# Gated linear attention with a small MLP on one core: centring the tokens before their transposes, a first pair in chunk halves, five phase products, another order table

## The chip, the cores and the metric

The kernel runs on one core of a Trainium2 chip. The time is the device time of one execution in microseconds, the median of several runs, lower is better. The core has a matrix engine (PE), a vector engine (DVE), a scalar engine for functions (ACT), a general engine (POOL), a queue engine that issues transfers (SP), and 16 DMA engines. Each engine has its own list of instructions, in the order in which the program gives them; what another engine has to finish first is waited for with semaphores.

## The reference

```python
# q, k, v, a_re, a_im: (4, 8, 768, 48) float32;  g_ln (384), w_ch1 (384, 1536), w_ch2 (1536, 384)
mag = sqrt(a_re**2 + a_im**2);  scale = minimum(mag, 0.999) / (mag + 1e-6)
a = (a_re + 1j * a_im) * scale
for t in range(768):                       # per batch and head, S is 48 x 48 complex
    S = a[t][:, None] * S + outer(k[t], v[t])
    y[t] = q[t] @ S.real
x = y with the heads side by side          # (4, 768, 384)
mu, var = mean(x), mean((x - mu)**2)       # per token, over 384
xn = (x - mu) / sqrt(var + 1e-6) * g_ln
out = x + maximum(xn @ w_ch1, 0) @ w_ch2
```

## The kernel before, in words

The time loop is gone: the product of gates between two steps is the exponential of a difference of running sums, of log magnitudes and of phases. The work is tiled in **chunks** of 128 tokens, six to a batch, 24 in all (`n`), and in **pairs** of two chunks, 12 in all (`P`, three to a batch). One pair goes through these steps; the names are those of the order table, `P` or `n` behind the dot:

- `are`, `aim`, `k`, `q`, `vf`: loads by SP. `wl.0` to `wl.5`: the two weight matrices, in thirds, by POOL's queue.
- `ln`, `iv`, `r`, `r2`, `u`, `l`, `lc`, `th`: log magnitude and phase of each gate, on ACT, DVE and POOL. `ln`, `iv`, `u`, `e`, `en` need ACT's table of logarithm and exponential, `th`, `sin`, `cos` the one of the trigonometric functions; `tab.log` and `tab.trig` load one or the other.
- `dec`: running sums of the log magnitudes, by products with a triangle of ones (`u_e`) on PE; `e` and `en` their exponentials with either sign. `ph`: the same for the phases (`u_th`), with the phase carried over from the pair before (`car`, picked out by `pick`); `sin`, `cos` (with `abs` or, in the first three pairs, `qt` ahead of it).
- `ke`, `qe`: k and q times the exponentials, `ks`, `qs`: those times cosine (`.0`) and sine (`.1`), on DVE or POOL.
- per chunk: `kT`, `qT` (transposes on PE) with the copies `ksT`, `qsT`, or one DMA transpose by SP in place of both; `am` the attention scores, `atm` the mask on DVE; `gm`, `G` the state; `y` the output, `x` its copy; `bn` mean and variance on DVE (two instructions); `xtr`, `xT` the transpose of the tokens and its copy.
- per pair: `mm1` (first MLP layer, 36 products of 256 columns in six steps), `relu`, `rstd`; per chunk `mm2` (second layer, 12 products of 384 columns in three steps), `oa`/`ot` (scaling and residual), `st` (store).

The mean of a token is not subtracted before: it is folded into the first weight matrix. `wgc` makes a 128 x 128 tile of g/384 (`gc`), `wp` multiplies the weights by it on PE, and `wc` writes g times weight minus that product back over the weights on DVE (L392), nine pieces, before the first `mm1`.

**The order is written out by hand:** `PLAN` is a table of some 1,000 tokens `step:engine+bank`, and each engine's instructions stand in the order of that table. The rings (`RINGS`) say how many buffers each tile has. `:G@step` puts a POOL step behind a step of DVE. `warm` steps are products without a use, which keep PE busy while nothing else is ready. Helpers hide the line of many operations: L293 is any elementwise product (`tt`), L288 and L290 a copy on ACT and DVE (`put`).

Lines of the profile: L449 loads of a_re, a_im; L452 `ln`; L454 `iv`; L466 `u`; L470, L473 `l`, `lc`; L481 `dec`; L485 `e`, `en`; L489 `th`; L507 `ph`; L533 `sin`; L544, L556 `cos`; L613 `kT`, `qT`; L618 their DMA form; L636 `am`; L664 `gm`; L686, L689 `y`; L699, L700 `bn`; L707 `xtr`; L741 `mm1`; L758, L760 `relu` on ACT and DVE; L773 `mm2`; L779, L789 the scaling; L806 `warm`; L811 `tab`.

## Time and profile before

| | us |
|---|---|
| median of 3 runs | 189.33 (188.43 to 190.59) |
| the profiled execution, whole | 189.38 |
| its span | 187.7 |
| busy PE / DVE / ACT / POOL | 175.9 / 159.0 / 156.0 / 95.7 |

The profiled execution took 1.7 us more than its span, which runs from the first to the last instruction. PE's busy time counts the latency of its pipelined products, so a full PE is not one at its peak: 36 products of the first layer are 269 to 283 ns each and follow each other in 109 ns. Of the 119 `warm` products in the trace all lie in its first 33 us.

### The profile page before, as it was taken

How to read it: one execution, taken by the hardware profiler on the slowest of the kernel's cores; microseconds unless marked ns; L12 is line 12 of the kernel's file. 1: busy time of each engine (PE TensorE's matmuls, PEld its weight loads, DVE VectorE, ACT ScalarE, POOL GpSimd, SP SyncE). 2: the span in 40 equal slices, each digit the busy share in tenths (PEclk: the TensorE clock that was granted, in tenths of full speed). 3: DMA queues.
4: the chain of work that ended last, by engine and by line, in shares of the span. 5: the costliest groups of instructions: out<-in, count | busy, mean ns of one | idle time of the engine just before them, and what ended most of it. 6: DMA issues, size and time to landing. Idle time of an engine off the chain costs nothing.

```text
span 187.7 us, 5141 instructions
## 1 busy us (share of the span) xinstructions
PE 175.9 (94%) x2040; PEld 138.6 (74%) x2040; DVE 159.0 (85%) x292; ACT 156.0 (83%) x223; POOL 95.7 (51%) x117
## 2 busy tenths in 40 slices
PE   5699999999999999999999999999999899797992
PEld 3488677888677897777877877877768577685772
DVE  0599999999989999889999899968999878676463
ACT  5699999999999999999999999988999869143220
POOL 8137387776614990696068570740621507521650
PEclk9999999999999999999999999999999999999999
DMA  5999999999999895899999999999989899996423
GB/s 136 284 243 178 235 237 213 209 191 227 228 235 265 188 263 131 147 219 213 187 244 206 181 245 218 179 227 171 213 188 197 190 210 155 234 121 167 136 98 126
DMA packets 131799, 37.23 MB, mean 198 GB/s; under 512 B 125888, under 2 KB 131776, under 8 KB 131776
## 3 DMA queue, kind: packets, MB, share of 16 engines
q1 hardware_dynamic: 128272, 33.76, 86.5%
q0 software_dynamic: 2784, 2.36, 8.5%
q10 hardware_dynamic: 720, 0.79, 1.2%
q8 instruction: 16, 0.26, 0.5%
q14 instruction: 7, 0.06, 0.1%
HBM read 28.31 MB, written 4.72 MB: 176 GB/s over the span
## 4 chain that ended last, share of the span: by engine, by line
PE 56%; DVE 19%; DMA 13%; issue 3%; SPq 3%; ACT 3%; POOL 1%; DVEq 0%; ACTq 0%; POOLq 0%
PE banks L773 20%; PE banks L741 14%; DMA aim<-in_a_im_dram 5%; DMA qsT<-qs 5%; PE banks L613 5%; PE banks L507 4%; PE banks L636 3%; DVE w1b L392 3%; DVE atm L293 3%; DMA ksT<-ks 2%; PE banks L481 2%; DVE r L293 2%; PE banks L686 2%; PE banks L707 2%; PE banks L689 2%
## 5 line engine op out<-in xcount | busy, mean ns | idle before, releaser
L773 PE MATMUL banks<-w2b,h 128*128 128x384 bf16 (+1 forms) x300 | 54.6, 319 | 0.0
L741 PE MATMUL banks<-xT,w1b 128*128 128x256 bf16 x432 | 51.2, 272 | 0.1
L741 PEld LDWEIGHTS <-w1b 128*128 128x128 bf16 x432 | 41.2, 98 | 6.5 <-DVE xT L290 0.8
L773 PEld LDWEIGHTS <-h 128*128 128x128 bf16 x300 | 26.8, 97 | 12.5
L293 DVE TENSOR_TENSOR atm<-banks,mask 128x1024 bf16<-128x1024 f32 x24 | 28.9, 1219 | 4.8 <-PE banks L636 4.5
L758 ACT ACTIVATE h<-banks 128x1024 bf16<-128x1024 f32 (+1 forms) x25 | 24.9, 1006 | 9.4 <-PE banks L741 9.2
L293 POOL TENSOR_TENSOR ke<-k,en 128x384 bf16<-128x384 f32 x17 | 15.8, 933 | 16.5 <-ACT en L485 4.7
L811 ACT ACT_TABLE_LOAD x18 | 23.1, 1283 | 1.1 <-PEq L827 0.8
L806 PE MATMUL banks<-u_e 128*128 128x256 f16 x119 | 16.7, 289 | 2.5 <-POOL u_e L322 2.2
L636 PE MATMUL banks<-qsT,ksT 128*128 128x128 bf16 x192 | 14.6, 219 | 2.9 <-DMA qsT<-qs 1.8
L760 DVE TENSOR_SCALAR h<-banks 128x1024 bf16<-128x1024 f32 (+1 forms) x12 | 14.0, 1175 | 3.7 <-PE banks L741 3.6
L293 POOL TENSOR_TENSOR qe<-q,e 128x384 bf16<-128x384 f32 x13 | 12.0, 929 | 9.3 <-DVE ks L293 5.3
L636 PEld LDWEIGHTS <-ksT 128*128 128x128 bf16 x192 | 12.2, 98 | 5.0 <-issue 2.3
L806 PEld LDWEIGHTS <-u_e 128*128 128x128 f16 x119 | 12.1, 104 | 4.6 <-POOL u_e L322 1.9
L293 POOL TENSOR_TENSOR r<-aim,are 128x768 f16<-128x768 f32 x6 | 10.9, 1813 | 6.1 <-ACT are L454 5.9
L786 POOL TENSOR_TENSOR ot<-ot,x 128x384 f32<-128x384 f32 x11 | 10.6, 974 | 6.3 <-DVE x L290 4.4
L288 ACT CAST x<-banks 128x384 bf16<-128x384 f32 x16 | 7.7, 483 | 7.2 <-PE banks L689 6.4
L470 DVE SCALAR_TENSOR_TENSOR l<-r,w 128x768 f16<-128x768 f16 (+1 forms) x13 | 12.9, 996 | 0.7 <-ACT r L466 0.6
L699 DVE BATCH_NORM_STATS2 stats<-x 128x6 f32<-128x384 bf16 x24 | 13.2, 550 | 0.3 <-ACT x L288 0.3
L293 POOL TENSOR_TENSOR qs<-qe,trig 128x768 bf16<-128x768 bf16 x6 | 10.3, 1725 | 5.9 <-DVE qe L293 3.5
L418 POOL TENSOR_SCALAR v<-vf 128x768 bf16<-128x768 f32 x8 | 7.0, 869 | 12.0 <-DMA vf<-in_v_dram 7.0
L686 PE MATMUL banks<-v,atm 128*128 128x48 bf16 x192 | 12.1, 183 | 0.2 <-DVE atm L293 0.2
(100 smaller groups left out, 385.0 us busy)
## 6 DMA issues: line engine op xcount, KB each, us to landing
k<-in_k_dram SPq DMA_DIRECT2D x24, 192.0 KB, 4.3
q<-in_q_dram SPq DMA_DIRECT2D x24, 192.0 KB, 4.5
vf<-in_v_dram SPq DMA_DIRECT2D x24, 192.0 KB, 4.1
are<-in_a_re_dram SPq DMA_DIRECT2D x11, 384.0 KB, 4.6
aim<-in_a_im_dram SPq DMA_DIRECT2D x11, 384.0 KB, 4.6
out_dram<-ot SPq DMA_DIRECT2D x20, 192.0 KB, 3.1
w1b<-in_moe_w_ch_dram POOLq DMA_DIRECT2D x3, 384.0 KB, 6.1
w2b<-in_moe_w_ch_dram POOLq DMA_DIRECT2D x3, 384.0 KB, 7.2
```

The costliest lines, as they stand in the source:

```text
L293: {"DVE": nc.vector, "POOL": nc.gpsimd}[eng(name)].tensor_tensor(**kw)
L470: nc.vector.scalar_tensor_tensor(out=S_("l"), in0=S_("r2"), scalar=0.5, in1=S_("w"), op0=ALU.mult, op1=ALU.add)
L636: nc.tensor.matmul(ps[:, h], lhsT=T("ksT", n)[:, h], rhs=T("qsT", n)[:, h], start=True, stop=True)
L686: nc.tensor.matmul(ps[:, h], lhsT=T("atm", n)[:, h], rhs=T("v", P)[:, c, h], start=True, stop=nfirst)
L699: nc.vector.bn_stats(out=T("stats", n), in_=T("x", n))
L741: nc.tensor.matmul(ps[:, jj], lhsT=w1b[:, dc, ts(gi * JG + jj, C)], rhs=T("xT", P)[:, dc].rearrange("p c t -> p (c t)"), start=(dc == 0), ...
L758: act(out=dst, in_=src, func=AF.Relu)
L760: nc.vector.tensor_scalar(out=dst, in0=src, scalar1=0.0, scalar2=None, op0=ALU.max)
L773: nc.tensor.matmul(bank(own)[:, 0:w], lhsT=T("h", P)[:, j, ts(c, C)], rhs=w2b[:, j, es], start=(j == 0), stop=(j == NJ - 1))
L786: nc.gpsimd.tensor_tensor(out=T("ot", n)[:, es], in0=T("ot", n)[:, es], in1=T("x", n)[:, es], op=ALU.add)
L806: g.add(f"warm.{i}", lambda i=i: nc.tensor.matmul(bank(f"warm.{i}")[:, 0:256], lhsT=u_e[:, 0, 0], rhs=u_e[:, 1].rearrange("p j t -> p (j t ...
L811: g.add(f"tab.{nm}.{i}", lambda tab=tab: nc.scalar.preload_act_table_set(tab))
```

## The change

1. **Centring.** A new step `xc` subtracts the token's mean (`mv`, from `bn`) from `x`, on DVE or POOL, and `xtr`/`xT` transpose `xc` in place of `x`. So a chunk's transpose now needs its `bn`. The weights are only scaled by g (`wg`, three instructions for each third: `wg.1` on DVE, `wg.0` on ACT, `wg.2` on POOL); `cmean`, `gc`, `wgc`, `wp` and `wc` are gone.
2. **Pair 0 by chunk.** Its two parts were heads 0 to 3 and 4 to 7; now they are chunk 0 and chunk 1. Its a_re and a_im come in runs of 192 bytes (384 before); its running sums take 3 and 5 products of 384 columns (8 and 12 of 192 before); its first layer is in 6 steps of 12 products of 128 columns, each with a `relu` of its own.
3. **Five phase products.** In pairs 1 to 11 one of the six products of `ph` is saved: a new step `tc` copies 64 rows of the phases into the tile of the carried phase, and one product with a joint matrix (`u_car`) does for two.
4. **A new order table.** 65 `warm` products of 256 columns and 57 of 512 (`warmw`) in place of 119 of 256. DMA transposes 28 in place of 25. Steps move between engines: for example `ks` is on DVE 16 times and on POOL 10 times (22 and 4 before), `qe` 6 and 18 (11 and 13 before); all nine `abs` are on ACT (7 before), seven of eight `car` too (4 of 9 before).

Where it moves instructions, at three places.

On ACT, between the table loads `tab.trig.3` and `tab.log.4`, ahead of the first MLP layer. Before:

```order
L811 ACT_TABLE_LOAD
L544 ACTIVATE trig_102<-banks 128x768
L533 ACTIVATE trig_103<-banks 128x768
L288 CAST G_128<-banks 128x384
L288 CAST x_132<-banks 128x384
L544 ACTIVATE trig_103<-banks 128x768
L288 CAST x_133<-banks 128x384
L489 ACTIVATE th_93<-r_84 128x768
L288 COPY qsT_122<-banks 128x1024
L811 ACT_TABLE_LOAD
```

The same stretch of ACT in the changed kernel (`r_88<-r_84` is `r2.3.0`, the square, `w1b<-w1b,gln` is `wg.0`):

```order
L877 ACT_TABLE_LOAD
L572 ACTIVATE trig_102<-banks 128x768
L508 ACTIVATE th_93<-r_84 128x768
L474 ACTIVATE r_88<-r_84 128x768
L290 CAST x_133<-banks 128x384
L561 ACTIVATE trig_103<-banks 128x768
L290 CAST x_132<-banks 128x384
L572 ACTIVATE trig_103<-banks 128x768
L398 ACTIVATE w1b<-w1b,gln 128x512 x3
L290 COPY qsT_122<-banks 128x1024
L877 ACT_TABLE_LOAD
```

The square of pair 3 (on POOL before) and the three scalings of the weights came into the stretch, the copy of the first state (`G_128`) left it for DVE.

On PE, the phases of pair 4 (`u_th` the triangle, `car` the carried phase). Before, six products, each with its load of weights:

```order
L507 LDWEIGHTS u_th
L507 MATMUL banks<-th_92,u_th 128x384
L507 LDWEIGHTS u_th
L507 MATMUL banks<-th_92,u_th 128x384
L507 LDWEIGHTS u_th
L507 MATMUL banks<-th_92,u_th 128x384
L507 LDWEIGHTS u_th
L507 MATMUL banks<-th_92,u_th 128x384
L507 LDWEIGHTS pick
L507 MATMUL banks<-car_167,pick 128x384
L507 LDWEIGHTS pick
L507 MATMUL banks<-car_167,pick 128x384
```

The same step in the changed kernel:

```order
L535 LDWEIGHTS u_th
L535 MATMUL banks<-th_92,u_th 128x384
L535 LDWEIGHTS u_th
L535 MATMUL banks<-th_92,u_th 128x384
L535 LDWEIGHTS u_th
L535 MATMUL banks<-th_92,u_th 128x384
L535 LDWEIGHTS u_car
L535 MATMUL banks<-car_170,u_car 128x384
L535 LDWEIGHTS pick
L535 MATMUL banks<-car_170,pick 128x384
```

One product less; the fourth one's phases now come by way of the carried tile.

On POOL, the end of the attention work (`ks_111` is pair 10, `ks_112` and `qe_109` pair 11, `qs_115` pair 11). Before:

```order
L293 TENSOR_TENSOR ks_111<-ke_106,trig_102 128x16x48
L293 TENSOR_TENSOR qe_108<-q_71,e_97 128x384
L418 TENSOR_SCALAR v_80<-vf_76 128x768
L293 TENSOR_TENSOR ke_107<-k_75,en_100 128x384
L786 TENSOR_TENSOR ot_166<-ot_166,x_136 128x384
L293 TENSOR_TENSOR ks_112<-ke_107,trig_103 128x16x48
L726 TENSOR_SCALAR rstd_155<-mv_150 128x2
L728 TENSOR_TENSOR rstd_155<-rstd_155,half_n 128x2
L786 TENSOR_TENSOR ot_165<-ot_165,x_135 128x384
L293 TENSOR_TENSOR qs_115<-qe_109,trig_103 128x16x48
```

In the changed kernel:

```order
L295 TENSOR_TENSOR qs_114<-qe_108,trig_102 128x16x48
L295 TENSOR_TENSOR ks_111<-ke_106,trig_102 128x16x48
L761 TENSOR_SCALAR rstd_157<-mv_152 128x2
L763 TENSOR_TENSOR rstd_157<-rstd_157,half_n 128x2
L295 TENSOR_TENSOR ks_111<-ke_106,trig_102 128x16x48
L848 TENSOR_TENSOR ot_169<-ot_169,x_136 128x384
L295 TENSOR_TENSOR ks_112<-ke_107,trig_103 128x16x48 x2
L761 TENSOR_SCALAR rstd_158<-mv_153 128x2
L763 TENSOR_TENSOR rstd_158<-rstd_158,half_n 128x2
L295 TENSOR_TENSOR qe_109<-q_72,e_98 128x384 x2
```

Five of the long products (128x16x48) of the last two pairs are on POOL where three were, and both `qe` of pair 11 stand behind them; before, these two were on DVE.

The core of the diff:

```diff
-         "ks": 3, "qs": 3, ... "x": 10, "stats": 4,
+         "ks": 3, "qs": 3, ... "x": 10, "xc": 3, "stats": 4,
 PLAN = """
-ue:G pickf:V qrow:G are.0.0:S tab.log.0:A ln.0.0:A pad.ks.2:G iv.0.0:A are.0.1:S aim.0.0:S r.0.0:V ln.0.1:A are.1.0:S
+are.0.0:S ue:G pick:G car0.1:G pad.ks.0:G tab.log.0:A ln.0.0:A pickf:V uth:V ucar:V aim.0.0:S are.0.1:S iv.0.0:A
...
+    def c_u0e():
+        nc.gpsimd.memset(u0_e, 1.0)
+        nc.gpsimd.affine_select(out=u0_e[:, 0], in_=u0_e[:, 0], pattern=[[1, C]],
+                                compare_op=ALU.is_ge, fill=0.0, base=0, channel_multiplier=-1)
+    def c_ucar():
+        for t, p in ((u_car, pick), (u_car_f, pick_f)):
+            nc.vector.tensor_copy(out=t[HALF:C], in_=p[HALF:C])
+            nc.vector.tensor_copy(out=t[0:HALF], in_=u_th[0:HALF, 0, 1])
...
-        def wp(jb=jb, o=o):
+        def f_wg(jb=jb):
             for dc in range(ND):
-                nc.tensor.matmul(bank(o), lhsT=gc[:, dc], rhs=w1b[:, dc, ts(jb, 512)],
-                                 start=(dc == 0), stop=(dc == ND - 1))
-        g.add(o, wp, needs=["wgc", f"wl.{jb}"], ps=(o, 1))
-        for ec in range(ND):
-            g.add(f"wc.{jb}.{ec}", lambda ...: nc.vector.scalar_tensor_tensor(
-                out=w1b[:, ec, ts(jb, 512)], in0=w1b[:, ec, ts(jb, 512)], scalar=gln[:, ds(ec, 1)],
-                in1=bank(o), op0=ALU.mult, op1=ALU.subtract), needs=[o], ps=(o, 1))
+                w = w1b[:, dc, ts(jb, 512)]
+                if eng(f"wg.{jb}") == "ACT":
+                    nc.scalar.mul(out=w, in_=w, mul=gln[:, ds(dc, 1)])
+                else:
+                    {...}[eng(f"wg.{jb}")].tensor_scalar(
+                        out=w, in0=w, scalar1=gln[:, ds(dc, 1)], scalar2=None, op0=ALU.mult)
+        g.add(f"wg.{jb}", f_wg, needs=[f"wl.{jb}", "gln"])
...
-            hs = ts(i, HS)
-            fs = ts(i, W)
+            hs = slice(0, H)
+            fs = slice(0, DM)
+            cr = slice(0, R) if NS == 1 else ds(i, 1)
...
+            if NS == 1:
+                def f_tc(X=X, fs=fs, step=step):
+                    dst, src = heads(T("car", P)[0:HALF, fs]), step(T("th", P), 1)[0:HALF]
+                    ...
+                add(f"tc.{X}", f_tc, needs=[f"th.{X}", f"car0.{P % RINGS['car']}"],
+                    uses=[("th", P), ("car", P)])
...
                             (0, u_th[:, 0, 0], th[0], True, False),
-                            (0, u_th[:, 0, 1], th[1], False, False),
                             (1, u_th[:, 1, 0], th[0], True, False),
                             (1, u_th[:, 1, 1], th[1], False, False),
-                            (0, w_car, car, False, True),
-                            (1, w_car, car, False, True)):
+                            (0, u_car_f if first else u_car, car, False, True),
+                            (1, pick_f if first else pick, car, False, True)):
...
+            def f_xc(n, c):
+                {"DVE": nc.vector, "POOL": nc.gpsimd}[eng(f"xc.{n}")].tensor_scalar(
+                    out=T("xc", n), in0=T("x", n), scalar1=T("mv", P)[:, c, 0:1], scalar2=None,
+                    op0=ALU.subtract)
+            add(f"xc.{n}", lambda n=n, c=c: f_xc(n, c), needs=[f"x.{n}", f"bn.{n}"],
+                uses=[("x", n), ("mv", P), ("xc", n)])
...
-                    nc.tensor.transpose(ps[:, dc], T("x", n)[:, ts(dc, C)], ident)
+                    nc.tensor.transpose(ps[:, dc], T("xc", n)[:, ts(dc, C)], ident)
...
-                needs=[f"xT.{P * R}", f"xT.{P * R + 1}"] + [f"wc.{gi}.{ec}" for ec in range(ND)],
+                needs=[f"xT.{P * R}", f"xT.{P * R + 1}"] + [f"wg.{gi}"],
```

More of the change, by code (lines that the diff above doesn't have):

```diff
@@ L808 @@
                 "p j t -> p (j t)"), start=True, stop=True), needs=["ue"], ps=(f"warm.{i}", 1))
+    for i in range(57):
+        g.add(f"warmw.{i}", lambda i=i: nc.tensor.matmul(
+            bank(f"warmw.{i}"), lhsT=u_e[:, 0, 0], rhs=u_e.rearrange("p c j t -> p (c j t)"),
+            start=True, stop=True), needs=["ue"], ps=(f"warmw.{i}", 1))
     for i in range(40):
```

386 lines of the change are left out of this document (212 added, 174 removed), and 2 rows, old and new, of the table RINGS.

## The prediction

> **What bounds the kernel now.** I read the page's head first, then the busy time by stage, then the chain that ended last. The stages are cut at the end of pair 0's first MLP layer (42.4), at 116 and at PE's last product (184.4).
>
> ```profile
> span 187.7 us, 5141 instructions
> ...
> 42.40:116.00 73.60, 73.46 (x869) 57.22 (x868) 69.73 (x130) 72.33 (x102) 42.33 (x40) 1.00 1.01 212
> 116.00:184.40 68.40, 65.00 (x744) 50.89 (x742) 53.80 (x94) 46.04 (x67) 27.31 (x30) 1.00 0.91 177
> 184.40:187.70 3.30, 0.00 (x0) 0.00 (x0) 0.40 (x1) 0.00 (x0) 0.00 (x0) 1.00 0.36 119
> ```
>
> The columns are the stage, its length, then PE, its weight loads, DVE, ACT and POOL. From 42.4 to 116 two engines are full at once: PE, 73.5 of 73.6, and ACT, 72.3. DVE has 4 us of air, POOL 31. After 116 all have some. How much of PE's busy time is work shows in the distance at which its products follow one another, here in pieces of the chain (start, length, what, how many):
>
> ```profile
> 46.82 0.89 PE banks L613 x16
> ...
> 58.18 0.98 PE banks L507 x6
> ...
> 64.32 0.20 PE banks L664 x8
> ...
> 98.53 1.95 PE banks L773 x12
> ...
> 176.47 3.94 PE banks L741 x36
> ```
>
> That is 0.163 us for 384 columns, 0.109 for 256, 0.055 for 128 and 0.025 for 48. With the counts of the program PE has 157 us of useful slots, and 13 of fillers. Counted along the table, 21.4 of the 157 are done at 42.4, so 135.7 are left for 142 us: PE lacks 6.2 us, only 1.3 of them before 116. The rest it waits behind 116, for this chain (rows of the chain and of the timeline):
>
> ```profile
> 121.75 5.85 DMA aim<-in_a_im_dram
> ...
> 157.27 0.85 ACT L556 ACTIVATE trig<-sh 128x768 bf16<-128x768 f16 x1
> 163.94 1.64 POOL L293 TENSOR_TENSOR qs<-qe,trig 128x768 bf16<-128x768 bf16 x1 [1.88 <-DVE qe L293]
> 166.06 3.54 SPq L618 DMA_TRANSPOSE qsT<-qs  x2
> 167.38 4.12 DMA qsT<-qs
> ...
> 171.65 0.61 PE banks L636 x8
> ...
> 180.42 3.94 PE banks L773 x36
> 184.38 0.42 DVE ot L789
> ```
>
> The cosine of pair 11 ends at 158.1, the DMA transposes of its products at 171.5, the last scores (`am.23`) at 172.1, and what PE has left behind them, 12.1 us, is dense. So the span is the end of the last cosine plus 29.6. ACT up to that cosine has 147.7 us of instructions, each counted at the distance at which such rows follow one another (0.70 to 0.80 for 768 columns, 0.92 for a `relu`, 0.4 for a copy of 384, 1.28 for a table): it lost 4.5 us before `tab.log.4` ended and 5.8 behind it, most of them after 116.
>
> **The head.** Here nothing is worth its own length; what counts is when ACT, the full engine, gets through.
>
> ```profile
> 3.52 0.52 ACT L452 ACTIVATE w<-are 128x384 f32<-128x384 f32 x1 [1.45 <-DMA are<-in_a_re_dram]
> ...
> 5.88 0.56 DVE L293 TENSOR_TENSOR r<-aim,are 128x384 f16<-128x384 f32 x1 [4.64 <-DMA aim<-in_a_im_dram]
> ...
> 6.87 0.52 ACT L466 ACTIVATE r<-r 128x384 f16<-128x384 f16 x1 [1.30 <-DVE r L293]
> ...
> 17.76 1.67 ACT L489 ACTIVATE th<-r 128x384 f16<-128x384 f16 x3
> ...
> 34.52 1.28 ACT L811 ACT_TABLE_LOAD   x1
> ...
> 35.37 1.47 PE L741 MATMUL banks<-xT,w1b 128*128 128x256 bf16 x12
> ...
> 180.51 0.60 ACT L758 ACTIVATE h<-banks 128x512 bf16<-128x512 f32 x1 [5.74 <-PE banks L741]
> ```
>
> The first `aim` is now issued second, not third. It lands between 4.5 (an issue of 0.5 and as much again after the first `are`, which was there at 3.5) and the old 5.8; I take 4.9, 0.9 earlier, as it has one load of its size ahead where it had two.
>
> ```profile
> k<-in_k_dram SPq DMA_DIRECT2D x24, 192.0 KB, 4.3
> ...
> are<-in_a_re_dram SPq DMA_DIRECT2D x11, 384.0 KB, 4.6
> ```
>
> The trace has 192 KB of `k`, in runs of 192 B, at 4.3 us to landing, and twice as much of `are`, in runs of 384 B, at 4.6: short runs are slow. The Trainium skill, DMA: Bandwidth & Descriptors (Specifications), agrees; it asks for 512 B and more for line rate, and so speaks against pair 0's shorter runs. By it the 0.9 would be lost again and the sum 0.9 higher.
>
> Half of the gain goes at once: `u.0.0` stands ahead of `ln.0.1` and `iv.0.1`, which filled the start of the gap of 1.3, and ACT has one square more (`r2.0.1`). Walking both lists with the durations of the rows, the phases begin at 17.5 for 17.76, and the third table load lies 0.35 earlier. Then come two stretches with more in them: `ln.4` and a copy for old ones (+0.7); then a square (0.75) and three scalings, which no row shows (0.5 each by the `relu` of 512 columns, 0.60 less overlap; between nothing and 0.6), less a state copy (0.4). `tab.log.4` begins at 37.0, 2.4 later. `am.2` stands ahead of the first MLP product on PE and needs the copy just ahead of that load, so this product starts at 37.5, for 35.4.
>
> PE however has less to do. Removed: `wp` 9 x 0.216 = 1.9, `ph` 11 x 0.163 = 1.8, three chunk transposes 24 x 0.055 = 1.3, and 0.3 in pair 0's sums. That makes 152 of 157. (The fillers, 6.5 us more, lie in these waits and push nothing in my walk; without them the head would be the same.) The first layer in steps of 128 columns costs the same slots. At 44.4 pair 0's first layer is through and 19.2 are done: 132.6 left, against 133.7 before at that time. **The head gains 1.1 us**, with 1.5 to either side for the walk.
>
> **DVE and POOL** have the large sums, and I give them almost nothing.
>
> ```profile
> L392 DVE SCALAR_TENSOR_TENSOR w1b<-w1b,gln,banks 128x512 bf16<-128x512 bf16 x9 | 6.3, 743 | 0.1
> ...
> L293 POOL TENSOR_TENSOR ks<-ke,trig 128x768 bf16<-128x768 bf16 x4 | 6.7, 1687 | 7.0 <-DVE ke L293 3.4 <-DVE r L293 2.3 <-DVE mv L700 1.2
> L293 DVE TENSOR_TENSOR ks<-ke,trig 128x768 bf16<-128x768 bf16 x18 | 9.7, 553 | 0.5 <-POOL ke L293 0.4
> L293 POOL TENSOR_TENSOR qe<-q,e 128x384 bf16<-128x384 f32 x13 | 12.0, 929 | 9.3 <-DVE ks L293 5.3 <-DMA q<-in_q_dram 2.0 <-DVE qs L293 1.6
> L418 POOL TENSOR_SCALAR v<-vf 128x768 bf16<-128x768 f32 x8 | 7.0, 869 | 12.0 <-DMA vf<-in_v_dram 7.0 <-DVE ot L789 2.6 <-DVE qsT L290 2.3
> L786 POOL TENSOR_TENSOR ot<-ot,x 128x384 f32<-128x384 f32 x11 | 10.6, 974 | 6.3 <-DVE x L290 4.4 <-ACT ot L779 1.9
> ...
> L728 POOL TENSOR_TENSOR rstd<-rstd,half_n 128x2 f32<-128x2 f32 x6 | 4.2, 707 | 0.5
> ...
> 8.01 0.26 DVE L473 TENSOR_SCALAR l<-l 128x384 f16<-128x384 f16 x1
> ...
> 41.24 0.56 DVE L699 BATCH_NORM_STATS2 stats<-x 128x6 f32<-128x384 bf16 x1
> 41.84 0.18 DVE L700 BATCH_NORM_AGGREGATE mv<-stats 128x2 f32<-128x6 f32 x1
> ```
>
> DVE loses `wc` (6.3) and `gc`, and work that goes to POOL; it gains 15 `xc` of 0.26 (by the `lc` row, the same size and kind): about -9 in all. POOL gains nine `xc` (0.45, half a `v`; at most 0.97, an `ot`), the scaling, six more `ks` of 1.69 and five more `qe`: about +22. DVE was not the last to be waited for before 116, so its 9 us buy little.
>
> `xc` also lengthens the way from `y` to `xtr`: `bn` (0.8, by the two rows) and `xc` come in, 1.1 to 1.3. PE work between the two hides it: the new table has 1.96 to 5.6 us there (the old one 0.8 to 3.4), and the way needs 0.17 of pipeline, 0.5 of copy, 0.8 and 0.26: 1.75. The smallest place is the last chunk, with 0.2 to spare. If that cover went everywhere, 22 times 1.1 is the bound.
>
> When DVE and POOL meet, one stands still:
>
> ```profile
> 18.27 0.97 DVE l L470
> ...
> 141.63 0.91 POOL L293 TENSOR_TENSOR ke<-k,en 128x384 bf16<-128x384 f32 x1 [2.40 <-ACT ot L779]
> ...
> 141.81 1.55 DVE L470 SCALAR_TENSOR_TENSOR l<-r,w 128x768 f16<-128x768 f16 x1
> ...
> 158.25 1.85 POOL L293 TENSOR_TENSOR ks<-ke,trig 128x768 bf16<-128x768 bf16 x1 [1.21 <-DVE mv L700]
> ```
>
> `l` takes 0.97 alone; begun under a POOL product it took 1.55, that is, it ran after POOL's end. The Trainium skill, SBUF — State Buffer (SBUF: two separate sides), says the same: the shared port pair is an exclusive lock for the whole instruction. By that rule POOL's 22 us more could cost DVE as much, and its gain of 9 would be a loss. I count nothing for it, since both still have air, but it is the reason for the third rival's stretch.
>
> **Middle and tail.** ACT's own list is not shorter: two `abs`, three `car`, two `tc`, one `v` and the scaling come, copies of states and transposes go; 147.8 up to the last cosine for 147.7. Having lost 3.8 by its table load (4.5 before), it can end that cosine at 151.6 plus later waits. With PE 1.1 ahead, ACT is the later one near pair 7: `mm2.15.0` asks for a `relu` that ends at 132.2 if ACT has lost 1.7 by then, and PE is there at 130.9: 1.3 of waiting. In the tail three things change. `aim.11` is issued 11 us of PE work earlier, so its landing of 5.85 is hidden. The last cosine stands ahead of the two `relu` that it had ahead. And the last transposes wait for POOL's run. From cosine to `am.23` I add: second `ks` 1.7, `rstd` 0.9 (0.71 and a short one ahead), two `qe` 1.8, two `qs` on DVE 1.0, two issues 2.6, landing 4.1, product 0.4: 12.5; then 12.7 of PE and 3.3: 28.5 for 29.6. With 4 us of ACT waits (5.8 before) the cosine ends at 155.6 and the span is 184.1.
>
> By PE: 44.4 + 132.6 + 1.3 (as before up to 116) + 1.3 (ACT) + 1.8 (tail, for 4.9) + 3.3 = 184.7. I take 184.6. The profiled execution lies 1.7 above its span (189.38), and equals the median (189.33): **186.3**.
>
> **Rivals.**
> - *ACT decides, and loses as much as before.* The cosine ends at 151.6 + 5.8 = 157.4, the span is 185.9, or 187 with PE's waits: 187.6 to 188.7; without the earlier `aim` up to 189.6. For it: ACT was full at equal load. Against: the late `aim.11` is gone.
> - *Nothing waits behind 116.* 44.4 + 132.6 + 1.3 + 0.5 + 3.3 = 182.1, time 183.8. For: DVE's 9 us. Against: the last DMA transposes can't start before the cosine.
> - *Slower: POOL's run in pairs 10 and 11.* From `sin.10` to the second `qe.11` POOL has 13 us in a row (five of 1.69, two `rstd`, `ot`, two `qe`), most of which was on DVE at 0.55. It decides once POOL comes to pair 11 after the cosine: then the first `ks` (1.7) and `ot` (1.0) join the 12.5, and five products at 1.85 add 0.8. With ACT's 157.4 the span is 157.4 + 28.5 + 3.5 = 189.4, the time 191.1. The port speaks for it; that POOL has 13 us from `sin.10` to the end, before PE comes, against.
> - *The centring isn't covered.* If half of the 22 transposes wait 0.5, that is 5.5: 191.8. The 1.96 and more of PE work speak against it.
>
> **How the numbers follow.** 1% of this time, 1.9 us, is about what a measurement tells from no change: 187.4 and 191.2 are the marks. The forecast (184.5 to 187.4) has 0.50, the rival without waits 0.08, ACT as before 0.27, the two slower ones together 0.15, a little of which stays within 1%. So faster 0.57, same 0.30, slower 0.13. The range leaves out the slower end and a part of the best case: 183.8 to 190.2.
>
> **What the profile after would show.** The first MLP product near 37.5 and `tab.log.4` near 37; PE without a gap over 0.5 us from 45 to 125; ACT's last cosine ending near 155.6; `am.23` near 168 and 16 us from it to the end; POOL 118 busy, DVE 150. A cosine after 159, or PE idle ahead of `xtr`, would make the prediction wrong.

## The result, and the profile after

| | before | after |
|---|---|---|
| median, us | 189.43 (188.43 to 190.59) | 201.63 (201.25 to 203.31) |
| ratio after to before, 95% interval | | 1.066 [1.057, 1.074] |
| profiled execution / its span, us | 189.38 / 187.7 | 203.31 / 201.3 |

The changed kernel is 12 us slower; 186.3, 3 us faster, was forecast. (Ratios here are always to the kernel before on the same chip and leave disturbed executions out, while the medians are of all, so the two differ a little.)

The head of the page after:

```profile
span 201.3 us, 5151 instructions
...
PE 182.3 (91%) x2021; PEld 135.0 (67%) x2021; DVE 162.0 (80%) x293; ACT 160.6 (80%) x231; POOL 127.8 (63%) x145
...
PE   5999789794899998799999979999989998998993
...
PEclk9999999999589999999999999999999999999998
```

DVE has 162.0 where 150 was forecast, POOL 127.8 for 118, and PE, which was to stand nowhere over 0.5 us from 45 to 125, has dents there (4 to 8 tenths in some slices of 5 us); at 50 to 60 its granted clock fell too. By stage, from the end of pair 0's first layer (54.5) to 130 and from there to PE's last product, with the columns as before:

```profile
54.50:130.00 75.50, 72.03 (x833) 54.77 (x832) 67.25 (x124) 68.41 (x101) 50.89 (x45) 0.98 0.95 194
130.00:197.90 67.90, 65.73 (x745) 50.13 (x742) 52.03 (x91) 47.24 (x67) 40.19 (x42) 1.00 0.85 172
```

Before, PE and ACT were both full in the first of these stages (1.3 us of air for ACT); now ACT has 7.1 us of air, PE 3.5 and DVE 8.3: no engine is full, they wait for one another. The groups that were new, with their mean in ns behind the busy time, and PE's transposes with what they waited for:

```profile
L733 POOL TENSOR_SCALAR xc<-x,mv 128x384 bf16<-128x384 bf16 x9 | 11.1, 1239 | 1.6 <-DVE mv L728 1.3 <-PE banks L717 0.3
...
L733 DVE TENSOR_SCALAR xc<-x,mv 128x384 bf16<-128x384 bf16 x15 | 6.4, 435 | 0.3
...
L400 POOL TENSOR_SCALAR w1b<-w1b,gln 128x512 bf16<-128x512 bf16 x3 | 4.7, 1566 | 0.0
...
L742 PE MATMUL banks<-ident,xc 128*128 128x128 bf16 x66 | 7.6, 228 | 6.7 <-POOL xc L733 6.1 <-DVE xc L733 0.6
```

An `xc` on POOL takes 1.24, not 0.45, nor within the 0.97 I gave as its most; one of `wg.2` 1.57. PE stands 6.1 us straight ahead of `xtr` (L742) for POOL. Where the time went is seen at three places. First the head, on ACT, DVE, POOL and PE in turn (timeline: start, length, what):

```profile
25.88 0.84 ACT L464 ACTIVATE w<-are 128x768 f32<-128x768 f32 x1 [1.22 <-DMA are<-in_a_re_dram]
...
30.51 1.28 ACT L877 ACT_TABLE_LOAD   x1
...
37.84 0.81 ACT L572 ACTIVATE trig<-banks 128x768 bf16<-128x768 int16 x1 [1.98 <-PE banks L568]
38.55 1.93 ACT L398 ACTIVATE w1b<-w1b,gln 128x512 bf16<-128x512 bf16 x3
...
41.40 1.28 ACT L877 ACT_TABLE_LOAD   x1
...
31.98 2.36 DVE L295 TENSOR_TENSOR atm<-banks,mask 128x1024 bf16<-128x1024 f32 x2 [0.21 <-PE banks L664]
34.26 2.15 DVE L295 TENSOR_TENSOR ks<-ke,trig 128x768 bf16<-128x768 bf16 x1
...
32.28 1.64 POOL L295 TENSOR_TENSOR qs<-qe,trig 128x768 bf16<-128x768 bf16 x1
...
34.35 1.63 POOL L295 TENSOR_TENSOR qs<-qe,trig 128x768 bf16<-128x768 bf16 x1
37.26 1.25 POOL L733 TENSOR_SCALAR xc<-x,mv 128x384 bf16<-128x384 bf16 x1 [1.28 <-DVE mv L728]
...
36.55 0.61 PE L641 MATMUL banks<-ident,ks 128*128 128x128 bf16 x8 [1.50 <-DVE ks L295]
...
41.90 1.50 PE L780 MATMUL banks<-xT,w1b 128*128 128x128 bf16 x24
```

`tab.trig.3` begins at 30.51, where the walk's terms (28.22 before, 0.35 earlier, 0.7 more work) give 28.6: 1.9 late, 1.22 of it ACT's wait for `are.3`. `tab.log.4` begins at 41.40, not 37.0, and the first MLP product at 41.90, not 37.5. In between DVE's `ks.1.0.0` and POOL's `qs.1.0.0` start 0.09 apart, and `ks` ends 0.43 after `qs` (36.41 and 35.98): 2.15 for the usual 0.55. `kT.3` on PE waits for it, `qt.2.0` stands behind `kT.3`, and ACT's cosine behind `qt.2.0`.

Then pair 0's first layer. First POOL, then PE:

```profile
42.69 4.65 POOL L400 TENSOR_SCALAR w1b<-w1b,gln 128x512 bf16<-128x512 bf16 x3
47.32 1.79 POOL L295 TENSOR_TENSOR r<-aim,are 128x768 f16<-128x768 f32 x1
49.10 2.46 POOL L733 TENSOR_SCALAR xc<-x,mv 128x384 bf16<-128x384 bf16 x2
...
47.40 0.73 PE L780 MATMUL banks<-xT,w1b 128*128 128x128 bf16 x10 [0.52 <-POOL w1b L400]
50.40 0.50 PE L742 MATMUL banks<-ident,xc 128*128 128x128 bf16 x3 [2.27 <-POOL xc L733]
51.62 0.50 PE L742 MATMUL banks<-ident,xc 128*128 128x128 bf16 x3 [0.72 <-POOL xc L733]
...
54.48 5.26 PE L803 MATMUL banks<-xT,w1b 128*128 128x256 bf16 x36
```

POOL does 8.9 us of work in a row, and PE waits at its end. Pair 0's first layer is through at 54.5, where 44.4 was forecast. At the end of the program (ACT, POOL, DVE, then PE):

```profile
169.01 0.84 ACT L584 ACTIVATE trig<-sh 128x768 bf16<-128x768 f16 x1
...
173.50 1.78 POOL L295 TENSOR_TENSOR qe<-q,e 128x384 bf16<-128x384 f32 x2
...
176.95 0.55 DVE L295 TENSOR_TENSOR qs<-qe,trig 128x768 bf16<-128x768 bf16 x1
...
184.32 0.61 PE L664 MATMUL banks<-qsT,ksT 128*128 128x128 bf16 x8
...
193.77 4.09 PE L835 MATMUL banks<-w2b,h 128*128 128x192 bf16 x36
```

The last cosine ends at 169.85 (155.6 forecast), `am.23` runs at 184.3 to 184.9 (168), the last product ends at 197.9 (181.3 by the sum that I took). So the sum of the miss, on PE: 4.4 us at the first MLP product, 5.7 more at the end of pair 0's first layer, 6.5 more from there to the end; together 16.6 (1.7 of them are that this execution was slower than its median). Of the last 6.5 at most 3.7 are waits ahead of `xtr` (6.7 less the 2.27 and 0.72 above) and 1.2 the slow clock behind 54.48 (5.26 for 4.09); the rest isn't assigned. Set against the kernel before, and not against the forecast, nearly all is lost in the head: pair 0's first layer ends 12.1 us later (54.5 for 42.4), the last product 13.5 later (197.9 for 184.4).

### The profile page after: what moved, and what is told of

Same layout as the page of the kernel before. It is cut to its first block, busy times and chain, and to the rows that moved or that the text cites. A ratio compares the mean times of both kernels' runs of the same rounds, so it can differ in the third digit from the quotient of the medians.

```text
span 201.3 us, 5151 instructions
## 1 busy us (share of the span) xinstructions
PE 182.3 (91%) x2021; PEld 135.0 (67%) x2021; DVE 162.0 (80%) x293; ACT 160.6 (80%) x231; POOL 127.8 (63%) x145
## 4 chain that ended last, share of the span: by engine, by line
PE 32%; DVE 17%; POOL 14%; SPq 13%; DMA 11%; ACT 6%; issue 5%; DVEq 0%; POOLq 0%
PE banks L835 11%; PE banks L803 10%; DMA vf<-in_v_dram 6%; SPq L414 6%; DVE atm L295 5%; POOL xc L733 4%; DMA ksT<-ks 4%; POOL r L295 4%; SPq L457 3%; SPq L646 2%; PE banks L664 2%; DVE ks L295 2%; DMA qsT<-qs 2%; POOL w1b L400 2%; PE banks L641 2%
## 5 line engine op out<-in xcount | busy, mean ns | idle before, releaser
L835 PE MATMUL banks<-w2b,h 128*128 128x384 bf16 (+1 forms) x300 | 54.5, 322 | 0.0
L803 PE MATMUL banks<-xT,w1b 128*128 128x256 bf16 x396 | 48.3, 276 | 0.1
L803 PEld LDWEIGHTS <-w1b 128*128 128x128 bf16 x396 | 38.4, 99 | 6.4 <-DMA xT<-xc 0.7
L820 ACT ACTIVATE h<-banks 128x1024 bf16<-128x1024 f32 (+1 forms) x23 | 23.0, 1003 | 10.5 <-PE banks L803 10.4
L295 POOL TENSOR_TENSOR qe<-q,e 128x384 bf16<-128x384 f32 x18 | 18.4, 1033 | 10.5 <-ACT e L504 6.0
L295 POOL TENSOR_TENSOR ke<-k,en 128x384 bf16<-128x384 f32 x15 | 14.2, 953 | 16.3 <-DVE r L295 7.5
L295 POOL TENSOR_TENSOR ks<-ke,trig 128x768 bf16<-128x768 bf16 x10 | 16.8, 1684 | 4.7 <-ACT trig L561 2.1
L872 PE MATMUL banks<-u_e 128*128 128x512 f16 x57 | 14.6, 414 | 2.2 <-POOL u_e L326 2.2
L742 PE MATMUL banks<-ident,xc 128*128 128x128 bf16 x66 | 7.6, 228 | 6.7 <-POOL xc L733 6.1
L424 POOL TENSOR_SCALAR v<-vf 128x768 bf16<-128x768 f32 x9 | 7.5, 829 | 8.2 <-DMA vf<-in_v_dram 4.2
L464 ACT ACTIVATE w<-are 128x768 f32<-128x768 f32 (+1 forms) x13 | 10.3, 790 | 3.0 <-DMA are<-in_a_re_dram 3.0
L872 PEld LDWEIGHTS <-u_e 128*128 128x128 f16 x57 | 6.0, 105 | 9.8 <-issue 2.9
```

Source lines behind the costliest of these rows:

```text
L295: {"DVE": nc.vector, "POOL": nc.gpsimd}[eng(name)].tensor_tensor(**kw)
L464: add(f"ln.{X}", lambda S_=S_: act(out=S_("w"), in_=S_("are"), func=AF.Ln), needs=[f"are.{X}"], uses=[("are", P), ("w", P)])
L803: nc.tensor.matmul(ps[:, jj], lhsT=w1b[:, dc, ts(gi * JG + jj, C)], rhs=T("xT", P)[:, dc].rearrange("p c t -> p (c t)"), start=(dc == 0), ...
L820: act(out=dst, in_=src, func=AF.Relu)
L835: nc.tensor.matmul(bank(own)[:, 0:w], lhsT=T("h", P)[:, j, ts(c, C)], rhs=w2b[:, j, es], start=(j == 0), stop=(j == NJ - 1))
L872: g.add(f"warmw.{i}", lambda i=i: nc.tensor.matmul(bank(f"warmw.{i}"), lhsT=u_e[:, 0, 0], rhs=u_e.rearrange("p c j t -> p (c j t)"), start ...
```

## The experiments

Three theories stood at the start. A: POOL's `xc` and `wg.2` are dear and PE waits for them. C: the centring lies on the way from `y` to `xtr`, on whichever engine. B, and D later: the new table is late as a whole. F came when the head had been read. The expectations count ACT's table loads without the one at the start: their third is `tab.trig.3`, their fourth `tab.log.4`.

### What an `xc` costs, and where it stands

```diff
# first: all nine           # second                # third: both
-xc.1:G ... xc.10:G         -wg.2:G                 
+xc.1:V ... xc.10:V         +wg.2:A                 
# fourth, for all 24 xc
-    scalar1=T("mv", P)[:, c, 0:1], scalar2=None, op0=ALU.subtract)
+    scalar1=0.0, scalar2=None, op0=ALU.subtract)
```

> The nine centrings `xc` that stand on POOL go to DVE, at the same places of the order table; all else as in the changed kernel. Theory A (the price of a POOL instruction whose scalar is a column of memory: 1.24 us each, 11.1 in all, which makes PE wait 6.1 us straight ahead of `xtr` and drop to about half its clock from 50 to 58): DVE does each in 0.26 to 0.44, PE's 6.1 us of idle time on `xc` fall below 1.5, the clock of 50 to 58 is whole again (some 2.5 us), and the time is 191 to 195. Theory B (the new order as a whole is late, by its head and by the transfers of SP; POOL's `xc` only stands where PE would have waited anyway): 198 to 201.6.

Measured: 199.35 against 189.09 as medians, with no interval; 195.89 and 198.42, the two lower of its four executions, are 1.036 and 1.050 of the kernel before (189.0). PE's waits for `xc` fell only from 6.7 us (POOL 6.1, DVE 0.6) to 3.9, now for DVE, whose 24 took 484 ns each. The clock of 50 to 60 was whole. A and C each hold in part.

> Only the scaling of the last third of the weights, `wg.2`, goes from POOL to ACT. Theory A: its 4.65 us, which stand ahead of `xc.3` and `xc.2` on POOL, become three of 0.71 on ACT; `xc.3` then runs near 46, the waits of 2.27 and 0.72 at 50.4 shrink to under 1 together, and the clock drop behind them goes: 196 to 199. Theory B: PE waits at the same place for something else (the relu of the first layer, or ACT, which is 2.1 later), 200 to 203.

Measured: 200.04, 1.056 [1.051, 1.062]; not apart from the changed kernel. The wait for `xc` shrank to 3.1, but with the scaling on ACT its `G` came 1.7 late for PE, and the clock fell there instead (0.83 in 40 to 50).

> Both moves together. Theory A: no instruction on POOL with a scalar from memory over 384 columns or more is left; 189 to 193, that is, most of the 12 us between the two kernels. Theory B: 197 to 201. What is left over 186.3 then is the late head (first MLP product at 41.9 where 37.5 was expected).

Measured: 198.44, 1.049 [1.043, 1.056]. Both moves give 1.7 points (hundredths of the ratio) of the 6.6; theory A alone had put nearly all there.

> All `xc` subtract the constant 0.0 in place of the token's mean (so the centring is left out), on the same engines at the same places. Theory A1 (the scalar from memory is what is dear on POOL): POOL's nine take 0.4 to 0.6 us each and the time is 193 to 197. Theory A2 (any instruction of this size is as slow on POOL, or it waits for DVE): they stay at 1.1 to 1.3 and the time stays within 199 to 202.

Measured: 198.79, 1.050 [1.045, 1.055], and A1 falls: without a scalar from memory POOL's `xc` still takes 1208 ns. What got better is that it no longer waits for `mv`. So the price belongs to the form of the instruction, which the next kernel takes apart:

> The changed kernel with eight of POOL's nine `xc` in other forms of 128x384 (some leave the centring out, one writes zeros): a copy; two operations with constants from bf16 and from f32; a subtraction with the mean and an addition of 0.0; one operation with a constant; one from f32; a subtraction with the mean spread over the row; one to f32 and a copy. Theory A3 (one operation alone takes a slower way on POOL than two, as `v` has two at 0.83 for 768): the forms with two operations take 0.4 to 0.5, those with one 1.2. Theory A4 (bf16 as the source is slow): all from bf16 1.2, all from f32 0.45. In either case the time is 198 to 203, and the durations are what is read.

Its one execution took 204.35, a little above the 198 to 203 expected. POOL's groups by form, sorted by the last number, the mean in ns:

```profile
L738 POOL COPY xc<-x 128x384 bf16<-128x384 bf16 x1 | 0.5, 493 | 0.0
L740 POOL TENSOR_SCALAR xc<-x 128x384 bf16<-128x384 bf16 x1 | 0.5, 502 | 0.0
L745 POOL TENSOR_SCALAR xc<-z 128x384 bf16<-128x384 f32 x1 | 0.5, 512 | 0.1
L751 POOL TENSOR_TENSOR xc<-x,mv 128x384 bf16<-128x384 bf16 x1 | 0.8, 827 | 0.3 <-PE banks L718 0.3
L749 POOL TENSOR_SCALAR xc<-x 128x384 bf16<-128x384 bf16 x1 | 1.2, 1169 | 0.0
L747 POOL TENSOR_SCALAR xc<-z,mv 128x384 bf16<-128x384 f32 x1 | 1.2, 1245 | 0.0
L742 POOL TENSOR_SCALAR xc<-x,mv 128x384 bf16<-128x384 bf16 x1 | 1.9, 1870 | 0.0
```

In order: a copy; times 1.0 plus 0.0, from bf16 and from f32; a subtraction of two tensors; times 1.0 alone; minus the mean, from f32; minus the mean plus 0.0. Neither A3 nor A4 holds: the source's type does nothing, and two operations with the mean cost more than one. Only copies and "times 1.0 plus 0.0" are cheap, and that pair is just what `v` (L424), my model for the price, uses. Whether any two constants would do, or only those that change nothing, wasn't tried.

```diff
# the cheapest form above that still centres, on POOL, with wg.2:A and qs.1.0.0:G@ks.1.0.0
+    nc.gpsimd.tensor_tensor(out=T("xc", n), in0=T("x", n), op=ALU.subtract,
+                            in1=T("mv", P)[:, c, 0:1].to_broadcast([C, DM]))
```

> The changed kernel with `wg.2` on ACT, POOL's `qs.1.0.0` behind DVE's `ks.1.0.0`, and the nine `xc` left on POOL in the form of a subtraction of two tensors, the mean spread over the row (0.83 each for 1.24). If the price of `xc` is what counts: within 1 of the same kernel with `xc` on DVE (196.75), 195.7 to 197.7, with PE's waits for POOL's `xc` below 2 us in all. If the meetings on the way count more than the price: 198 to 200.

Measured: 195.89 on a chip where the kernel before took 191.53: 1.024 [1.013, 1.035], the best of all versions of the changed kernel that compute the whole; the same kernel with `xc` on DVE had 1.036 [1.028, 1.045], and the intervals overlap. POOL's `xc` had a mean of 859 ns, and PE waited 0.6 us for it, in a profiled execution of 202.97 us, the longest of the five. So in the cheap form `xc` on POOL is not worse than on DVE; that it is better isn't shown.

### What the centring and the scaling cost in all

```diff
# first: no xc              # second: no wg either
-xc.0:G xc.1:G ...          -wg.1:V wg.0:A wg.2:G
-transpose(ps[:, dc], T("xc", n)[:, ts(dc, C)], ident)
+transpose(ps[:, dc], T("x", n)[:, ts(dc, C)], ident)
```

> The changed kernel without its 24 `xc`: the transposes read `x` again, so the mean is not subtracted at all; scaling, table and all else stay. Theory C (the centring stands on the way from `y` to `xtr`, on either engine, and is not covered): the 8 us in which PE stands ahead of `xtr` go, the clock of 50 to 58 is whole, only the late head (first MLP product at 41.9, some 4.4 late) is left: 190 to 193. Theory D (the waits at `xtr` only take the place of others, because DVE's or ACT's lists are as late): 195 to 199, the same as with `xc` on DVE.

Measured: 196.40, 1.023 [1.012, 1.035]: the centring, POOL's price for it included, is worth 4.3 points of 6.6, about 8 us. This is the largest single part, though the ratio rests on two executions. By the ratio the time is 194.6, between the ranges of C and D. Most of it shows at one place: pair 0's first layer ends at 48.8 for 54.5.

> As the kernel without centring, and without the scaling of the weights by g as well (both left out). It prices `wg`: ACT loses 1.9 us between its third and fourth table load, DVE 2.0 and POOL 4.65 in the head. If `wg` makes the head late: first MLP product about 2 us earlier and 188 to 191, some 2 below the kernel without centring. If the head is late by its order and by the loads of SP: within 0.7 of the kernel without centring.

Measured: 194.24, 1.018 [1.010, 1.026], not apart from the kernel without centring, and the first MLP product came no earlier (42.43 for 41.40). Here `ks` took 2.67, and behind PE's wait for it the clock fell to 0.50 at 38 to 40, which cost about 1.1 us (an estimate: 6.43 from the end of that wait to the first MLP product, for 5.33 without centring alone). Less that, the product comes at the same time: `wg` isn't what makes the head late.

### The meeting of `ks` and `qs`

```diff
-qs.1.0.0:G
+qs.1.0.0:G@ks.1.0.0
```

> The changed kernel with one token more: POOL's `qs.1.0.0` waits for DVE's `ks.1.0.0`, so that the two products no longer run into one another at 34.3. Theory F (DVE stands while POOL's product runs: `ks` takes 2.15 there, 0.55 alone; `kT.3` on PE stands 1.65, `cos.2.0` on ACT 1.98 behind it): `ks` takes 0.55 to 0.7, PE's gap of 1.65 falls below 0.5, the fourth table load of ACT begins 1 to 1.6 earlier (39.8 to 40.4), and the time is 1 to 2.5 below the changed kernel's: 199 to 200.6. Theory G (DVE and POOL don't disturb one another, `ks` waits for something else, or the gap only moves): 201 to 203.

DVE and POOL of that kernel:

```profile
34.82 0.55 DVE L295 TENSOR_TENSOR ks<-ke,trig 128x768 bf16<-128x768 bf16 x1
...
35.45 1.65 POOL L295 TENSOR_TENSOR qs<-qe,trig 128x768 bf16<-128x768 bf16 x1 [0.67 <-DVE ks L295]
37.07 1.26 POOL L733 TENSOR_SCALAR xc<-x,mv 128x384 bf16<-128x384 bf16 x1
```

`ks` is back at 0.55, PE's wait is gone, and ACT's fourth table load begins 1.0 earlier (40.38), all as theory F has it; but the time is 201.15, 1.062 [1.057, 1.067], in the range of G. `xc.1` on POOL, behind the `qs` that now starts later, begins at 37.07 for 37.26, and the first MLP product at 41.70 for 41.90. The gain of DVE was given to a list that was as late. Where POOL has no `xc` behind it, the same token counts:

> The changed kernel with all `xc` on DVE, `wg.2` on ACT and POOL's `qs.1.0.0` behind DVE's `ks.1.0.0`; it computes all. Theory F: now POOL has no `xc` behind its `qs`, so the token counts: the fourth table load begins 1 to 2 earlier than at 41.2, and the time is 195.5 to 197 (198.4 without the token). Theory G: 198 to 199.5.

Without the token (first) and with it (second), DVE's product and ACT's `tab.log.4`:

```profile
33.72 2.47 DVE L295 TENSOR_TENSOR ks<-ke,trig 128x768 bf16<-128x768 bf16 x1
...
41.19 1.28 ACT L877 ACT_TABLE_LOAD   x1
```

```profile
34.06 0.55 DVE L295 TENSOR_TENSOR ks<-ke,trig 128x768 bf16<-128x768 bf16 x1
...
39.61 1.28 ACT L877 ACT_TABLE_LOAD   x1
```

Measured: 196.75 for 198.44; 1.036 [1.028, 1.045] for 1.049 [1.043, 1.056], two intervals that just overlap. The spans of the two profiles differ by 2.7 (194.7, 197.4). The mechanism of theory F holds, and the time lies in its range. In this kernel without the token, in the changed one, and in those without centring and without centring and scaling, `ks` ends 0.42 to 0.43 after POOL's `qs`. The Trainium skill, SBUF — State Buffer (SBUF: two separate sides), has a DVE product of two SBUF tensors contend with POOL's reads, and the one that comes second stands for the whole instruction. That one of the two stands agrees (2.47 against 0.55), and so do the two `atm` above, which read their scores from PSUM and kept 1.18 each beside POOL's first `qs`. That it is the second doesn't come out: by the profile, whose times on POOL are rough, `ks` began 0.09 ahead of `qs` in the changed kernel and 0.41 ahead of it in this one.

> The kernel without centring and without scaling (both left out), and with POOL's `qs.1.0.0` behind DVE's `ks.1.0.0`. Without the token `ks` took 2.67 and PE stood 2.2 us at 36.0. Theory F: `ks` 0.55, that gap below 0.5, the first MLP product near 40 (42.4 without the token), and the time 190.5 to 192.5 (194.2 without it). Theory G (another list is as late here too): 193.5 to 195.

Measured: 193.05, 1.014 [1.007, 1.020] (1.018 without the token, intervals overlap). `ks` took 0.66, and the first MLP product came at 39.62 for 42.43, as theory F has it; but the profiles' spans are the same (191.0 and 191.1), since PE then stood 1.6 us ahead of 48.2 for DVE's `xT` of pair 1.

> As the kernel with `xc` on DVE, `wg.2` on ACT and `ks` first, and the ten `ks` that stand on POOL go to DVE (0.55 each there, 1.7 on POOL). Theory L (DVE's short products stand while POOL's long ones run, 14 us of lengthened rows in all): DVE's 5.5 us more are paid by fewer meetings, the lengthened time falls below 9, and the time is 193 to 196. Theory M (DVE's own list is the late one before `xtr`): 0.5 to 3 slower than the kernel it is made from.

Measured: 197.97, 1.039 [1.031, 1.046]: no gain, and theory M's sign within the noise. DVE's short products were held up less (`xc` 355 ns in the mean for 467; how far the lengthened time as a whole fell isn't known), but behind 60 us PE's waits for `xc` only fell from 1.3 to 1.1, and those for DMA transposes rose from 1.3 to 2.4.

### The head's loads, and the clock

```diff
-vf.0.1:S ... q.1.1:S ... are.3.0:S ... vf.0.0:S        # first: on the kernel with ks first
+vf.0.1:S vf.0.0:S q.1.1:S ... are.3.0:S
+warm.65:P2 ... warm.82:P2                              # second: in the changed kernel, ahead of xtr.3
```

> As the kernel with `xc` on DVE, `wg.2` on ACT and `ks` first, and the load `vf.0.0` is issued two loads earlier, straight behind `vf.0.1`. If the late landing of `vf` (26.6; POOL stands 4.2 us for it, PE 0.9 to 1.4 behind POOL) holds the head: `v.0` begins 1 to 2 us earlier and the time falls by 0.7 to 1.5. If the load of `are.3` behind it (ACT stands 1.2 for it) becomes as late: no change, within 0.5.

Measured: 199.78, 1.051 [1.046, 1.057]: 3 us slower. Of POOL, ACT and DVE:

```profile
25.14 0.95 POOL L424 TENSOR_SCALAR v<-vf 128x768 bf16<-128x768 f32 x1 [2.11 <-DMA vf<-in_v_dram]
...
27.05 0.84 ACT L464 ACTIVATE w<-are 128x768 f32<-128x768 f32 x1 [1.90 <-DMA are<-in_a_re_dram]
...
30.05 2.25 DVE L295 TENSOR_TENSOR r<-aim,are 128x768 f16<-128x768 f32 x1 [0.43 <-ACT are L466]
```

`v` did come 1.6 earlier (26.75 without the move), but `are.3` landed later (`ln.3` begins at 27.05 for 26.00), and DVE's `r.3.0`, 1.05 long before, now lay beside POOL's `qe` (30.56 to 31.49) and took 2.25. `ks` began 1.9 later. One token of SP's list made a new meeting.

> The changed kernel with 18 products without a use (0.109 each, 1.96 us in all) straight ahead of `xtr.3` on PE, where it stands 2.3 us for POOL's `xc`. If the fall of the clock costs what it seems (the 36 products of pair 1's first layer took 5.26 from 54.48, where 36 such take 4.1 later): they take 4.1 to 4.3, the granted clock of 50 to 60 is above 0.9 (0.66 without the products), and the time is 1 to 2.5 below 201.6. If the clock falls for another reason: 201 to 203.

The windows of 50 to 60 (PE, its loads, DVE, ACT, POOL, then PE's clock), of the changed kernel and of the filled one:

```profile
50.00:60.00 10.00, 8.88 (x61) 6.77 (x62) 6.64 (x13) 6.59 (x9) 5.36 (x6) 0.66 1.09 226
```

```profile
50.00:60.00 10.00, 9.27 (x100) 7.82 (x101) 9.12 (x16) 8.80 (x15) 6.65 (x7) 1.00 1.06 228
```

The clock is whole and the 36 products take 4.09 for 5.26, as expected; the wait as such stays. Yet the time is 204.43 where the kernel before took 191.53: 1.067 [1.057, 1.076], as without. So PE's standing still causes the fall. At its place the fall costs some 2.7 us (from `xtr.3` to the end of pair 1's first layer, waits not counted, 8.5 for 5.8), but nothing of it reached the end in these runs: behind 140 the filled kernel stood 3.7 us for DMA transposes, the changed one 1.7. The Trainium skill, TensorE: Matmul & The Clock Gate (What's actually happening), has the clock halve after an idle window of about 3.4 us. The half agrees: in windows of 1 us the changed kernel's clock is 0.50 from 51 to 56. The length doesn't: the wait of 2.27 alone was enough, as the three products right behind it took 0.50 where three such take 0.34 at full clock. Nor does the length of a wait decide by itself: in the kernel with only `wg.2` on ACT one of 2.14 (to 36.5) left the clock whole, and one of 1.65 (to 45.0) was followed by 0.50 from 47 to 49.

### Parts of the change alone, in the kernel before

```diff
# first                                   # second
-x.0:A1 ... xtr.0:P6 ... bn.0:V            -x.0:A1 ... xtr.0:P6 ... bn.0:V
+x.0:A1 bn.0:V xc.0:V ... xtr.0:P6         +x.0:A1 ... bn.0:V xc.0:V xtr.0:P6
-wgc:V wp.1:P4 wc.1.2:V4 wc.1.1:V4 wc.1.0:V4 ...
+wg.1:V ...
```

> The kernel before with one part of the change alone: `bn` and `xc` (all 24 on DVE) stand straight behind `x`, the transposes read `xc`, the weights are only scaled, on DVE, where the first `wc` of each third stood; order, pair 0, phase products and engines of all else as before. Theory C: the old table has 0.8 to 3.4 us of PE work between `y` and `xtr` where the way needs 1.75, so several transposes wait 0.5 to 1: 191 to 196. Theory E (centring as such is cheap, and the new table is what costs): 186 to 189.5.

> As the kernel before with centring, but `bn` and `xc` stand straight ahead of `xtr` in the order table and not straight behind `x`, so that DVE does other work while `x` is copied on ACT. Theory H (the 51 us came from DVE standing in line for `x`, with PE waiting and its clock falling): the time falls to 195 to 215, since DVE waits less but `xtr` stands right behind `xc`. Theory I (any `xc` on the way costs this much in this table): 230 to 245.

Measured: 241.21, 1.265 [1.254, 1.275], and 229.98, 1.207 [1.201, 1.213]. PE's waits ahead of `xtr` in the two (total, times, longest):

```profile
PE banks L700 <- DVE xc L691: 21.3, 16, 3.1
```

```profile
PE banks L700 <- DVE xc L691: 24.4, 20, 2.4
```

C and E both missed the first by far, and for the second I's range holds, not H's. Three instructions of 1.3 in all (0.55, 0.18 and an `xc` of 0.54 to 0.59 in the mean), of which only `xc` is new on DVE's list and `bn` stands earlier, cost 40 to 51 us: in the second kernel 20 of the 22 transposes wait 1.2 in the mean, and PE's clock was 0.92 and 0.96 over the two runs. The waits and the clock don't make the whole sum; that what PE gives later is then late for DVE and ACT as well is how I read the rest, and wasn't tried. So the new table hides much more of the centring than the old one does. With `xc` on DVE and `ks` first in the changed kernel the same row reads:

```profile
PE banks L742 <- DVE xc L733: 2.1, 5, 0.6
```

Then the five phase products alone:

```diff
+ucar:V tc.1.0:V ph.1.0:P6      # tc at eleven such places; ucarf ahead of tc.3.0
-(0, u_th[:, 0, 1], th[1], False, False),
-(0, w_car, car, False, True),
+(0, u_car_f if first else u_car, car, False, True),
```

> The kernel before with the five phase products alone: `tc` on DVE straight ahead of `ph`, two joint matrices made in the head; all else as before. PE loses 11 products (1.8 us), DVE has 11 copies of 0.24 more. If the saving counts in full: 187.3. If `tc` delays `ph` behind DVE's list: 190 to 193. I expect 189.0, within 1%, since PE waits in the tail for the last cosine and not for its own work.

Measured: 198.64, 1.048 [1.044, 1.052]. I missed by 9.6 us: the eleven copies took 0.67 each, not 0.24, and cost more than the products saved, because `ph` now stands for them at the end of DVE's list (the copies, then PE's wait for them):

```profile
L291 DVE COPY car<-th 64x384 f16<-64x384 f16 x11 | 7.3, 666 | 0.0
...
PE banks L526 <- DVE car L291: 8.2, 9, 2.2
```

> The kernel before with one token moved: the load `aim.11` is issued straight behind `are.11`, some 12 us earlier. By the term of the prediction (the chain of the last cosine passes through its landing of 5.85 at 121.75) the last cosine comes earlier and the time falls by 1 to 2: 187.3 to 188.4. If the chain has another wait right behind it (ACT's own list): 188.8 to 189.6.

Measured: 189.56, 1.001 [0.998, 1.005]: nothing, the expectation's second case by the time, though the wait behind it is not on ACT's list. Of DVE, in the kernel before and then with the earlier load:

```profile
127.68 0.96 DVE L293 TENSOR_TENSOR r<-aim,are 128x768 f16<-128x768 f32 x1 [0.53 <-DMA aim<-in_a_im_dram]
```

```profile
128.48 0.56 DVE L418 TENSOR_SCALAR v<-vf 128x768 bf16<-128x768 f32 x1 [1.67 <-DMA vf<-in_v_dram]
```

The landing of `aim.11` stood in the chain with 5.85 us, but DVE stood only 0.53 for it. With the earlier load that wait is gone, yet the `v` straight ahead on DVE's list waits 1.67 for `vf` (0.94 before), and `r.11` begins no earlier (128.96).

## Why the prediction was wrong

Both signs came that the prediction had named for being wrong: a cosine after 159 (169.85), and PE idle ahead of `xtr` (6.7 us).

- **The price of `xc` and `wg` on POOL: the step that failed first.** "0.45, half a `v`; at most 0.97, an `ot`": `v` was the nearest row by name, but it is a form of its own. Nine `xc` at 1.24 for 0.45 are 7.1 of the 10 us by which POOL's list is longer than forecast (127.8 for 118); for `wg.2` (three of 1.57) the prediction names no price on POOL. Moving both off POOL gave 1.7 points of the 6.6, with `ks` first as well 3.0, and with the cheap form on POOL 4.2 (1.024).
- **"PE work between the two hides it": failed.** The way of 1.75 was worked out for DVE at 0.26 (0.435 in the mean) and an empty list. Whatever the cover, `xc` waited in POOL's list behind `wg.2`, `r.4` and `qs`. Leaving the centring out gave 4.3 of the 6.6 points. The rival "the centring isn't covered" came nearest, at 191.8, and its mechanism was the right one (5.5 us of waits ahead of `xtr`; 6.7 measured); I gave it a part of 0.15.
- **"I count nothing for it" (DVE and POOL standing for one another): failed at one place.** One meeting took `ks` from 0.55 to 2.15 or more and counts about 1.3 points where nothing hides it (by two intervals that just overlap). Taking POOL's `ks` away in the later stages bought nothing.
- **DVE's 9 us less: not there.** DVE has 162.0 for 159.0 before. `wc` and `gc` went (7.6 us by their groups), but `xc` took 6.4 for the 3.9 forecast, and `tc` (2.1) and `wg.1` (2.0) stand in no sum of the prediction.
- **The head's gain of 1.1: lost, 4.4 of the 16.6.** I walked ACT's list alone. It lost 1.9 up to `tab.trig.3`, 1.22 of them for a load that the walk took as landed, and 2.5 behind it, since its cosine hangs on PE, PE on DVE and DVE on POOL (1.98), and `wg.0` took 1.93 for 1.5. (The walk's own terms add up to 2.2 later, not to the 2.4 that it takes.) By the rule of the Trainium skill, DMA: Bandwidth & Descriptors (Specifications), that transfers below 512 B miss line rate, the 0.9 of the earlier `aim` would be lost again. The trace doesn't show that: the first `r` on DVE begins at 4.92 (4.9 forecast, 5.88 before) and waits last for ACT, whose first `are` lands 0.29 later than before (3.81 for 3.52).
- **The tail: 31.5 from cosine to end for 28.5.** The two `qs` on DVE began at 176.95, 1.7 behind the last `qe`, as DVE's list was late. That `aim.11` is hidden was counted as a gain; in the kernel before it was worth nothing: the 5.85 us were the length of a landing, of which DVE stood 0.53, and the wait for `vf` ahead of it took over.
- **The likeliest rival, ACT as before, didn't come:** ACT has 7 us of air where it had 1.3. Nor did POOL's run in pairs 10 and 11: POOL itself waited 2.07 us for pair 11's sine, ahead of 169.21.
- **PE's shorter list** came (by the distances above its rows sum to about 152, as forecast), and behind the head it seems to have turned into time. By one profiled execution of each kernel, in us:

| | pair 0's first layer ends | PE's last product ends | between |
|---|---|---|---|
| before | 42.4 | 184.3 | 141.9 |
| changed | 54.5 | 197.9 | 143.4 |
| without centring | 48.8 | 188.3 | 139.5 |
| without centring and scaling | 49.3 | 187.3 | 138.0 |
| the same, `ks` first | 46.4 | 187.2 | 140.8 |
| forecast | 44.4 | 181.3 | 136.9 |

With centring, scaling and the meeting all gone the kernel is still 1.4% [0.7, 2.0] above the one before, where the forecast had even the whole kernel 1.6% below. By the table this rest lies in the head: 4.0 us late at the end of pair 0's first layer, 2.0 of which the forecast had, and 1.1 less than before from there on (differences of 1 to 2 us are within the scatter of single executions). What makes the head late stays open. It isn't POOL's `xc`, the scaling or the one meeting; its first MLP product (39.62) is 2.1 behind the walk's 37.5. No version tried here beats the kernel before.

## What to carry to other kernels

A row is a price only for its own form: "the same engine, the same size, the same name" was off by 2.8 times, and one kernel with an instruction in each form settles it. When a step is put between a producer and an engine that has no air, work out when the engine that does it comes to it, behind everything ahead in its list, not how long it takes. And an engine's list can't be walked alone in a head where four lists hang on each other: take a late step out, and the next one in line takes the gain. Nor is a landing in the chain that ended last a price: the wait for it can be much shorter, and another can stand beside it.
